# Retention attention and a mixture of adapters: each transfer of the SyncE queue waits for the landing of the third one ahead, and keys come in 256 KB pieces

## The chip, the cores and the metric

The kernel runs on one core of a Trainium2 chip. The metric is the device time of one execution in microseconds; lower is better. The median of the runs before the change is 192.85 us (three runs, 192.42 to 196.5).

## What is computed

The inputs are q, k and v of shape (8 batches, 8 heads, 576 positions, 64), all float32. Attention has no softmax; a decay per head takes its place:

```python
scores = q @ k.T / sqrt(64)                       # per batch and head, 576 x 576
D[i, j] = gamma[h] ** (i - j) if i >= j else 0    # gamma[h] = 1 - 2 ** (-5 - h)
x = (scores * D) @ v                              # heads laid side by side: 4608 rows of 512
logits = x @ w_gate                               # 8 experts, the best two are kept
out = x + sum over the two of w * ((x @ A[e]) @ B[e])     # A: 512 x 16, B: 16 x 512
```

Since D is a product of a factor of i and a factor of j, each block of rows needs only the keys and values of its own block and a 64 x 64 state per head that sums all earlier blocks.

## The kernel before

**Units.** The work is cut into 18 units (`units`). Units 0 to 15 are a pair of batches (bp) and a block c of 128 positions; units 16 and 17 are four batches each with the last 64 positions. The four units of one c come one after the other, so a state `SP[bp]` is used again four units later.

**Loads.** `load(u, w)` brings the tile of one unit from HBM into a buffer of `nt`: 512 KB for each of k, q and v. Before the change a key tile of units 1 to 15 is one transfer of 512 KB (line 160), values are two of 256 KB (line 148), queries from unit 2 on are two of 256 KB (line 153), and the tiles of units 16 and 17 are two of 256 KB each (line 144). Unit 0 comes in halves by batch (`load_batch`, line 538). Rows of k and v are 256 bytes in HBM; those of the paired q are 512. There are five buffers for q and six each for k and v.

**The SyncE queue.** All loads and nearly all stores are issued by SyncE, in the order in which the program writes them. First come units 0, 1 and 2, the expert weights (`AW`, lines 556 and 560: four transfers of 64 KB and one of 16 KB), and then units 3, 4 and 5. From then on `ahead(t)` sets the order:

```python
def ahead(t):
    for u in {4: (0,), 5: (1, 2)}.get(t, (t - 3,)):
        if t > 3 and has(u):
            store(u)                 # two stores of 256 KB, line 525
    for w in "kqv":
        load(t + 4, w)               # k, then q, then v
    if has(t + 1):
        first_state(t + 1)           # two copies on GpSimd, line 316
    if has(t + 2):
        scale_(t + 2, "k", pool2)    # line 179, GpSimd, one instruction a batch
        if t > 2:
            scale_(t + 2, "q", pool2)
```

The transfers before already carry a wait for the eighth one ahead of them, because eight semaphores are used in turn, and waits for their buffers.

**A round.** From t = 5 on each pass of the loop at the end does, on TensorE in this order: `scores(t)` (ps_s, line 269), `logits(t-1)` (pz, line 393), `small(t-2)` (pzt, line 378), `sums(t+1)` (pu, line 300), the transposes of k and q of unit t+1 (lines 215 and 202), `back(t-2)` (po, line 459), `products(t)` (px, line 350) and `output(t-2)` (po, line 475). GpSimd does `routing_4(t-2)` (cm and zc, lines 441 and 443) first, and then what `ahead(t)` gives it. ScalarE empties PSUM; VectorE masks. The engines' order is the program's; a semaphore wait at the head of an engine holds all that is behind it.

Of the kernel before, what the change touches and what calls it, by code (L numbers as in the profile page):

```python
# [18 lines left out]
def kernel(  # L19
# [10 lines left out]
    nc = tc.nc  # L30
    B, H, S, Dh = q.shape
# [31 lines left out]
    for c in range(NFULL):  # L63
# [9 lines left out]
    dr_pack2 = nc.inline_tensor(pack2_np, "c_pack2")  # L73
# [12 lines left out]
    pack2 = cpool.tile([128, NP2], FP32, tag="pack2", name="pack2", align_bytes=256)  # L86
# [14 lines left out]
        cpool.tile([128, 2, HP, Dh], FP32, tag=f"SP{bp}", name=f"SP{bp}") for bp in range(NP)  # L101
    ]

    units = [(c, bp) for c in range(NFULL) for bp in range(NP)] + [
        (NFULL, qd) for qd in range(NQ)
    ]
    NU = len(units)
# [4 lines left out]
    def paired(u):  # L112
        return 1 < u < NU and units[u][0] < NFULL
# [6 lines left out]
    def nt(u, w):  # L120
        if (u, w) not in nat:
            shape = [128, 2, 2 * H, Dh] if w == "v" else [128, 2 * H, Dh]
            nat[(u, w)] = iop.tile(
                shape, FP32, tag=w + "32", name=w + "32", bufs=5 if w == "q" else 6,
                align_bytes=256,
            )
        return nat[(u, w)]

    def block(u, t):
        return nt(u, "v")[:, t]  # L130

    def rows(w, b0, nb, s0, n):
        return SRC[w][b0 : b0 + nb, :, s0 : s0 + n, :].rearrange("b h j d -> j (b h) d")

    def load(u, w):
        if u >= NU:
            return
        c, bp = units[u]
        s0 = 128 * c
        if c == NFULL:  # L140
            for t in range(2):
                hf = slice(64 * t, 64 * t + 64)
                dst = block(u, t)[hf] if w == "v" else nt(u, w)[hf]
                nc.sync.dma_start(out=dst, in_=rows(w, 4 * bp + 2 * t, 2, s0, 64))
        elif w == "v":
            for t in range(2):
                hf = slice(64 * t, 64 * t + 64)
                nc.sync.dma_start(  # L148
                    out=block(u, t)[hf], in_=rows(w, 2 * bp, 2, s0 + 64 * t, 64)
                )  # L150
        elif w == "q" and paired(u):
            for b in range(2):
                nc.sync.dma_start(
                    out=nt(u, w)[64 * b : 64 * b + 64].rearrange("p (h e) d -> p h (e d)", e=2),
                    in_=q[2 * bp + b, :, s0 : s0 + 128, :].rearrange(
                        "h (p e) d -> p h (e d)", e=2
                    ),
                )
        else:
            nc.sync.dma_start(out=nt(u, w), in_=rows(w, 2 * bp, 2, s0, 128))  # L160

    def scale_(u, w, engines, bs=(0, 1)):
        c, _ = units[u]
# [356 lines left out]
    def store(u):  # L520
        c, bp = units[u]
        of = st.pop(u)["osb"].rearrange("p b a o d -> p b (a o d)")
        for b in range(2):
            if c < NFULL:
                nc.sync.dma_start(
                    out=o3[2 * bp + b, 128 * c : 128 * c + 128, :], in_=of[:, b]
                )
            else:
                for t in range(2):
                    (nc.gpsimd if b and u == NU - 2 else nc.sync).dma_start(  # L530
                        out=o3[4 * bp + 2 * t + b, 128 * c : 128 * c + 64, :],
                        in_=of[64 * t : 64 * t + 64, b],
                    )


    def load_batch(u, w, b):
        c, bp = units[u]
        nc.sync.dma_start(  # L538
            out=nt(u, w)[:, b * H : b * H + H], in_=rows(w, 2 * bp + b, 1, 128 * c, 128)
        )  # L540

# [4 lines left out]
    for b in range(2):  # L546
        for w in "kq":
            load_batch(0, w, b)
    load(0, "v")
    for w in "kqv":  # L550
        load(1, w)
    nc.sync.dma_start(out=pack2, in_=dr_pack2.ap())
    for w in "kqv":
        load(2, w)
    for dt in range(HP):
        nc.sync.dma_start(  # L556
            out=AW[:, dt, 0:ER].rearrange("p (e r) -> p e r", e=E),
            in_=moe_A[:, 128 * dt : 128 * dt + 128, :].rearrange("e d r -> d e r"),
        )
    nc.sync.dma_start(  # L560
        out=AW[:, :, ER : ER + E],
        in_=moe_w_gate.rearrange("(t p) e -> p t e", p=128),
    )
# [66 lines left out]
# [3 lines that stand above are left out]
                store(u)  # L633
        for w in "kqv":
            load(t + 4, w)
        if has(t + 1):
            first_state(t + 1)
        if has(t + 2):
            scale_(t + 2, "k", pool2)
            if t > 2:  # L640
                scale_(t + 2, "q", pool2)
# [51 lines left out]
    def finish():  # L693
        u = NU - 1
        s = st[u]
        store(u - 3)
        routing_4(u - 2)
        scores(u)
# [6 lines left out]
        routing_4(u - 1)  # L705
        products(u)
        store(u - 2)

        bv = Bcat.rearrange("p (a o d) -> p a o d", a=HP, o=2)
# [8 lines left out]
        for b in range(2):  # L718
# [10 lines left out]
                out=ns, in0=m8[:, 0:1], scalar=-1.0, in1=m8[:, 1:2],  # L729
# [3 lines left out]
                out=ge, in0=z[:, ER : ER + E],  # L733
# [3 lines left out]
                out=sg, in_=z[:, ER : ER + E], func=AFT.Sigmoid, bias=ns, scale=2.0  # L737
# [3 lines left out]
                out=c.rearrange("p (e r) -> p e r", e=E),  # L741
# [21 lines left out]
        def output_b(b, zt):  # L763
            o = mo.tile([128, HP, 2, 64], FP32, tag=f"oe{b}", name="oe", bufs=1, align_bytes=256)
            for ho, eng in ((0, nc.scalar), (1, nc.vector)):
                nc.tensor.matmul(
                    po[b][ho], lhsT=zt, rhs=bv[:, :, ho, :],
                    start=False, stop=True, skip_group_check=True,
                )
                (eng.copy if eng is nc.scalar else eng.tensor_copy)(  # L770
                    out=o[:, :, ho, :], in_=po[b][ho]
                )
            c, qd = units[u]
            of = o.rearrange("p a o d -> p (a o d)")
            for t in range(2):
                (nc.scalar if b and t else nc.sync).dma_start(
                    out=o3[4 * qd + 2 * t + b, 128 * c : 128 * c + 64, :],
                    in_=of[64 * t : 64 * t + 64],
                )

        zt0 = small_b(0)
        for b, tag in ((0, "s"), (1, "x")):
# [3 lines left out]
            for dt in range(HP):  # L786
                for ho in range(2):
# [3 lines left out]
                        is_transpose=True, start=(dt == 0), stop=False, skip_group_check=True,  # L791
                    )
        output_b(0, zt0)
        output_b(1, small_b(1))

    stage_A(2)
# [104 lines left out]
```

## Time and profile before

| | |
|---|---|
| median of the runs | 192.85 us (192.42 to 196.5, three runs) |
| profiled execution, its own time | 190.79 us |
| its span, first to last instruction | 188.9 us |
| granted TensorE clock, mean | 0.986 |
| busy: TensorE / VectorE / ScalarE / GpSimd | 167.3 / 113.3 / 114.1 / 108.7 us |
| HBM read, written | 29.02 MB, 9.44 MB |
| packets of the SyncE and ScalarE queues (q1) | 81.1% of 16 DMA engines' span |

The span is one execution as the hardware profiler recorded it; the execution's own time is 1.9 us longer, for what lies before the first and after the last instruction. "SPq" is SyncE's queue: its rows show how long each transfer held the issuing engine, which includes its waiting, and not how long the data took. A transfer's time to landing runs from the start of its issue to the last update of its semaphore.

### The profile page before, as it was taken

How to read it: one execution, taken by the hardware profiler on the slowest of the kernel's cores; microseconds unless marked ns; L12 is line 12 of the kernel's file. 1: busy time of each engine (PE TensorE's matmuls, PEld its weight loads, DVE VectorE, ACT ScalarE, POOL GpSimd, SP SyncE). 2: the span in 40 equal slices, each digit the busy share in tenths (PEclk: the TensorE clock that was granted, in tenths of full speed). 3: DMA queues.
4: the chain of work that ended last, by engine and by line, in shares of the span. 5: the costliest groups of instructions: out<-in, count | busy, mean ns of one | idle time of the engine just before them, and what ended most of it. 6: DMA issues, size and time to landing. Idle time of an engine off the chain costs nothing.

```text
span 188.9 us, 10441 instructions
## 1 busy us (share of the span) xinstructions
PE 167.3 (89%) x4675; PEld 148.9 (79%) x4675; DVE 113.3 (60%) x227; ACT 114.1 (60%) x255; POOL 108.7 (58%) x162
## 2 busy tenths in 40 slices
PE   3989598799889889898999999999997999999960
PEld 3578498588879788788999989899996988988840
DVE  1384837665296475748577787777594846555240
ACT  3437163735569484765767868494959394674650
POOL 1333321567769988493949586675969397520240
PEclk9999969999999999999999999999999999999998
DMA  7999969999999999999999999999998853112325
GB/s 157 248 221 225 227 70 232 202 224 246 224 228 235 262 252 277 252 260 247 241 257 246 266 232 250 221 278 226 271 206 243 181 169 115 50 68 111 115 56 166
DMA packets 108075, 38.99 MB, mean 206 GB/s; under 512 B 88768, under 2 KB 103488, under 8 KB 108032
## 3 DMA queue, kind: packets, MB, share of 16 engines
q1 hardware_dynamic: 107568, 37.71, 81.1%
q8 instruction: 36, 0.59, 1.4%
q0 software_dynamic: 240, 0.39, 1.0%
q10 hardware_dynamic: 224, 0.24, 0.5%
q14 instruction: 7, 0.06, 0.1%
HBM read 29.02 MB, written 9.44 MB: 204 GB/s over the span
## 4 chain that ended last, share of the span: by engine, by line
PE 59%; SPq 14%; issue 7%; DMA 6%; POOL 5%; DVE 4%; ACT 2%; POOLq 0%; ACTq 0%
PE px L350 15%; PE pz L393 12%; PE ps_s L269 8%; PE pu L300 6%; PE po L475 5%; PE po L459 4%; PE pt_k L215 4%; SPq L148 3%; SPq L556 3%; PE pt_q L202 3%; DMA k<-in_k_dram 3%; SPq L160 3%; DMA q<-in_q_dram 3%; POOL k L179 2%; SPq L538 2%
## 5 line engine op out<-in xcount | busy, mean ns | idle before, releaser
L179 POOL TENSOR_TENSOR k<-k,pack 128x512 f32<-128x512 f32 x32 | 34.9, 1109 | 17.4 <-DMA k<-in_k_dram 16.5
L350 PE MATMUL px<-x,v 128*64 128x64 f32 (+1 forms) x576 | 39.3, 226 | 2.6 <-DVE x L289 0.8
L289 DVE TENSOR_TENSOR x<-ps_s,pack 64x512 f32<-64x512 f32 (+1 forms) x38 | 25.1, 660 | 25.9 <-PE ps_s L269 25.6
L350 PE MATMUL px<-qT,v 128*64 128x64 f32 (+1 forms) x576 | 39.2, 226 | 1.3 <-DVE qT L289 1.1
L350 PEld LDWEIGHTS px<-x,v 128*64 128x64 f32 (+1 forms) x576 | 36.2, 140 | 4.4 <-ACT kT L240 1.0
L350 PEld LDWEIGHTS px<-qT,v 128*64 128x64 f32 (+1 forms) x576 | 36.1, 140 | 1.9 <-DVE qT L289 1.2
L393 PE MATMUL pz<-AW,xT 128*128 128x136 f32 x272 | 36.1, 286 | 0.6 <-ACT kT L240 0.6
L393 PEld LDWEIGHTS pz<-AW,xT 128*128 128x128 f32 x272 | 32.6, 190 | 1.8 <-ACT kT L240 0.8
L169 POOL TENSOR_TENSOR qs<-q,pack 128x512 f32<-128x512 f32 x25 | 26.1, 1062 | 4.1 <-DMA q<-in_q_dram 4.1
L406 ACT COPY zs<-pz 128x272 f32<-128x272 f32 x17 | 6.6, 386 | 33.2 <-PE pz L393 32.5
L289 DVE TENSOR_TENSOR qT<-ps_s,pack 64x512 f32<-64x512 f32 (+1 forms) x38 | 25.1, 660 | 1.1
L269 PE MATMUL ps_s<-qT,kT 64*64 64x64 f32 x1152 | 23.6, 224 | 2.1 <-issue 1.4
L269 PEld LDWEIGHTS ps_s<-qT,kT 64*64 64x64 f32 x1152 | 20.4, 137 | 6.2 <-issue 3.1
L441 POOL TENSOR_TENSOR cm<-ge,sg 128x16 f32<-128x16 f32 x17 | 4.0, 234 | 36.5 <-PE pt_k L215 16.9
L316 POOL COPY v<-SP 64x512 f32<-64x512 f32 x32 | 20.5, 640 | 1.6
L300 PE MATMUL pu<-v,k 64*64 64x64 f32 x1024 | 19.2, 221 | 0.8 <-DMA v<-in_v_dram 0.8
L240 ACT COPY kT<-pt_k 128x512 f32<-128x512 f32 x34 | 18.2, 589 | 1.2 <-PE pt_k L215 1.0
L253 DVE COPY x<-qT 64x512 f32<-64x512 f32 x17 | 14.5, 852 | 7.4 <-ACT qT L235 5.0
L366 ACT COPY xT<-px 128x512 f32<-128x512 f32 x28 | 16.3, 625 | 4.4 <-PE px L350 4.4
L300 PEld LDWEIGHTS pu<-v,k 64*64 64x64 f32 x1024 | 16.9, 134 | 2.5 <-DMA v<-in_v_dram 0.9
L492 ACT COPY osb<-po 128x512 f32<-128x512 f32 x33 | 17.6, 584 | 1.0 <-PE po L475 1.0
L252 DVE COPY x<-qT 64x512 f32<-64x512 f32 x14 | 8.1, 579 | 16.0 <-ACT qT L235 12.0
(68 smaller groups left out, 242.6 us busy)
## 6 DMA issues: line engine op xcount, KB each, us to landing
v<-in_v_dram SPq DMA_DIRECT2D x36, 256.0 KB, 5.2
q<-in_q_dram SPq DMA_DIRECT2D x34, 256.0 KB, 5.2
out_dram<-osb SPq DMA_DIRECT2D x32, 256.0 KB, 4.2
k<-in_k_dram SPq DMA_DIRECT2D x15, 512.0 KB, 5.7
k<-in_k_dram SPq DMA_DIRECT2D x6, 256.0 KB, 4.3
q<-in_q_dram SPq DMA_DIRECT2D x1, 512.0 KB, 6.9
out_dram<-oe SPq DMA_DIRECT2D x3, 128.0 KB, 3.3
AW<-in_moe_A_dram SPq DMA_DIRECT2D x4, 64.0 KB, 3.6
```

The costliest lines, as they stand in the source:

```text
L169: engines[b].tensor_tensor(out=qs[:, :, 4 * b : 4 * b + 4, :].rearrange("p e h d -> p h e d"), in0=tl[:, b * H : b * H + H, :].rearrange(" ...
L179: engines[b].tensor_tensor(out=tl[:, b * H : b * H + H, :], in0=tl[:, b * H : b * H + H, :], in1=g[:, c, :].unsqueeze(2).broadcast_to((128 ...
L240: nc.scalar.copy(out=tl[:, r], in_=st[u]["p" + w][r])
L253: eng.tensor_copy(out=x2[0:64, 1, b], in_=qT[64:128, 1, b])
L269: nc.tensor.matmul(ps[ho][64 * t : 64 * t + 64, b, hp, :], lhsT=kT[sl, t, b, hp, :], rhs=qT[sl, t, b, hp, :], start=(hp == 0 and b == bs[0 ...
L289: nc.vector.tensor_tensor(out=out, in0=in0, in1=m, op=ALU.mult)
L300: nc.tensor.matmul(pu[t][64 * ho : 64 * ho + 64, b, hp, :], lhsT=kn[sl, h, :], rhs=block(u, t)[sl, h, :], start=(hp == 0 and b == 0), stop ...
L316: copy(out=dst[:, :, :, ho, :], in_=src[64 * ho : 64 * ho + 64])
L350: nc.tensor.matmul(px[b][64 * ho : 64 * ho + 64, hp, t, :], lhsT=block(u, t)[rw, b * H + 2 * hp + ho, :], rhs=facing(u, t, ho)[rw, b, hp, ...
L366: nc.scalar.copy(out=xt.rearrange("p a (t i e) -> p (a t) e i", t=2, e=2), in_=px.rearrange("p a t (e i) -> p (a t) e i", e=2),)
L393: nc.tensor.matmul(pz[:, b, :], lhsT=st[u]["xT"][b][:, dt, :], rhs=AW[:, dt, :], start=(dt == 0), stop=(dt == HP - 1), skip_group_check=True,)
L492: copy(out=s["osb"][:, :, :, ho, :], in_=s["po"][ho])
```

## The change

A helper `move` issues every transfer of SyncE, keeps them in a list, and from the fourth on adds a wait for the landing of the transfer three places earlier in that list. So at most three transfers of this queue are on the way at a time. Key tiles (and the one q tile of unit 1 that takes the same branch) are issued as two transfers of 256 KB, one a batch, in place of one of 512 KB. Transfers issued by ScalarE (the first constants, one store at the end) and GpSimd (`Bcat`, two stores at the end) are not in the list.

```diff
+    inflight = []
+
+    def move(out, in_):
+        dma = nc.sync.dma_start(out=out, in_=in_)
+        if len(inflight) >= 3:
+            tc.add_manual_dep(
+                dma.ins, inflight[-3].ins.name,
+                mybir.DependencyInfo(mybir.DependencyClass.Sync, mybir.DependencyReason.DATA),
+                reason="pace",
+            )
+        inflight.append(dma)
...
         else:
-            nc.sync.dma_start(out=nt(u, w), in_=rows(w, 2 * bp, 2, s0, 128))
+            for b in range(2):
+                move(
+                    out=nt(u, w)[:, b * H : b * H + H], in_=rows(w, 2 * bp + b, 1, s0, 128)
+                )
...
             if c < NFULL:
-                nc.sync.dma_start(
+                move(
                     out=o3[2 * bp + b, 128 * c : 128 * c + 128, :], in_=of[:, b]
                 )
             else:
                 for t in range(2):
-                    (nc.gpsimd if b and u == NU - 2 else nc.sync).dma_start(
+                    (nc.gpsimd.dma_start if b and u == NU - 2 else move)(
```

All other `nc.sync.dma_start` calls become `move` in the same way. The order of instructions on TensorE, VectorE, ScalarE and GpSimd stays as it was. SyncE has 151 transfers in place of 135. In the changed program the instruction that scales the second batch of a key tile waits for the second key transfer alone, and the first for the first.

More of the change, by code (lines that the diff above doesn't have):

```diff
@@ L143, in load @@
                 dst = block(u, t)[hf] if w == "v" else nt(u, w)[hf]
-                nc.sync.dma_start(out=dst, in_=rows(w, 4 * bp + 2 * t, 2, s0, 64))
+                move(out=dst, in_=rows(w, 4 * bp + 2 * t, 2, s0, 64))
         elif w == "v":
@@ L152, in load @@
             for b in range(2):
-                nc.sync.dma_start(
+                move(
                     out=nt(u, w)[64 * b : 64 * b + 64].rearrange("p (h e) d -> p h (e d)", e=2),
@@ L159, in load @@
         else:
-            nc.sync.dma_start(out=nt(u, w), in_=rows(w, 2 * bp, 2, s0, 128))
+            for b in range(2):
+                move(
+                    out=nt(u, w)[:, b * H : b * H + H], in_=rows(w, 2 * bp + b, 1, s0, 128)
+                )
     def scale_(u, w, engines, bs=(0, 1)):
@@ L524, in store @@
             if c < NFULL:
-                nc.sync.dma_start(
+                move(
                     out=o3[2 * bp + b, 128 * c : 128 * c + 128, :], in_=of[:, b]
@@ L537, in load_batch @@
         c, bp = units[u]
-        nc.sync.dma_start(
+        move(
             out=nt(u, w)[:, b * H : b * H + H], in_=rows(w, 2 * bp + b, 1, 128 * c, 128)
@@ L551 @@
         load(1, w)
-    nc.sync.dma_start(out=pack2, in_=dr_pack2.ap())
+    move(out=pack2, in_=dr_pack2.ap())
     for w in "kqv":
@@ L555 @@
     for dt in range(HP):
-        nc.sync.dma_start(
+        move(
             out=AW[:, dt, 0:ER].rearrange("p (e r) -> p e r", e=E),
@@ L559 @@
         )
-    nc.sync.dma_start(
+    move(
         out=AW[:, :, ER : ER + E],
@@ L775, in output_b @@
             for t in range(2):
-                (nc.scalar if b and t else nc.sync).dma_start(
+                (nc.scalar.dma_start if b and t else move)(
                     out=o3[4 * qd + 2 * t + b, 128 * c : 128 * c + 64, :],
```

## The prediction

> **What bounds the kernel now.** I read the page first, then busy time by stage, the chain in order of time, SyncE's timeline and GpSimd's. The page:
>
> ```profile
> span 188.9 us, 10441 instructions
> PE 167.3 (89%) x4675; PEld 148.9 (79%) x4675; DVE 113.3 (60%) x227; ACT 114.1 (60%) x255; POOL 108.7 (58%) x162
> q8 instruction: 36, 0.59, 1.4%
> PE 59%; SPq 14%; issue 7%; DMA 6%; POOL 5%; DVE 4%; ACT 2%; POOLq 0%; ACTq 0%
> ```
>
> TensorE is busy 89% of the span, but a fifth of the chain that ended last (SPq and DMA) is transfers. Where these lie is shown by busy time in three stretches (columns: stretch, its length, then PE, PEld, DVE, ACT, POOL busy, granted clock, DMA share, GB/s) and by the chain (start, length, what):
>
> ```profile
> 0.00:55.00 55.00, 45.47 (x1232) 38.60 (x1232) 30.64 (x60) 26.71 (x58) 22.86 (x36) 0.97 0.96 209
> 55.00:150.00 95.00, 90.41 (x2711) 82.62 (x2713) 65.53 (x127) 65.24 (x144) 70.27 (x96) 1.00 0.98 244
> ...
> 26.74 5.68 DMA k<-in_k_dram
> 32.48 0.86 POOL k L179
> ...
> 44.00 5.15 DMA q<-in_q_dram
> ...
> 52.38 1.50 issue
> ...
> 109.47 1.10 PE ps_s L269 x64
> 118.02 0.49 PE ps_s L269 x18
> 121.61 0.11 PE pzt L378 x2
> ```
>
> Until some 50 us the chain runs through SyncE's queue and landings: the key issued at 26.74 lands at 32.42 and GpSimd scales it at 32.48. After 55 us it is TensorE alone, one round each 118.02 - 109.47 = 8.55 us. But the transfers are hardly slower than that, as a round of SyncE's queue shows (start, time that the issues held SyncE, what):
>
> ```profile
> 106.66 0.46 SPq L160 DMA_DIRECT2D k<-in_k_dram  x1
> 107.22 3.79 SPq L153 DMA_DIRECT2D q<-in_q_dram  x2
> 111.11 2.45 SPq L148 DMA_DIRECT2D v<-in_v_dram  x2
> 113.66 1.64 SPq L525 DMA_DIRECT2D out_dram<-osb  x2
> 115.34 0.46 SPq L160 DMA_DIRECT2D k<-in_k_dram  x1
> ...
> L153 SPq DMA_DIRECT2D q<-in_q_dram x28: 627/1436/3217, 15.4 to 127.7; - x28
> ```
>
> A round of transfers takes 115.34 - 106.66 = 8.68 us and SyncE never rests: a q issue takes 0.63 us unhindered and up to 3.2 us here. So the queue is full and transfers flow at 8.68 us a round against TensorE's 8.55. How far they are ahead is in GpSimd's timeline:
>
> ```profile
> 117.05 2.28 POOL L179 TENSOR_TENSOR k<-k,pack 128x512 f32<-128x512 f32 x2
> 119.29 2.04 POOL L169 TENSOR_TENSOR qs<-q,pack 128x512 f32<-128x512 f32 x2
> 123.56 0.22 POOL L441 TENSOR_TENSOR cm<-ge,sg 128x16 f32<-128x16 f32 x1 [2.23 <-PE pt_k L215]
> 123.86 0.77 POOL L443 TENSOR_TENSOR zc<-zs,cm 128x128 f16<-128x128 f32 x2
> ...
> k<-in_k_dram SPq DMA_DIRECT2D x15, 512.0 KB, 5.7
> v<-in_v_dram SPq DMA_DIRECT2D x36, 256.0 KB, 5.2
> q<-in_q_dram SPq DMA_DIRECT2D x34, 256.0 KB, 5.2
> out_dram<-osb SPq DMA_DIRECT2D x32, 256.0 KB, 4.2
> ```
>
> The key issued at 106.66 lands about 5.7 us later, at 112.4, and is scaled at 117.05: a lead of 4.7 us. Behind it GpSimd rests 2.2 us before cm, and that zc, done at 124.6, feeds the pzt of the next round, at 121.61 + 8.55 = 130.2: another 5.6 us. So keys and queries may come 4.7 + 2.2 + 5.6 = 12.5 us later, here, before TensorE waits. Before 50 us there is no such cover.
>
> **The change part by part.** *The wait.* Landing times of a round add up to 5.7 + 2 x 5.2 + 2 x 5.2 + 2 x 4.2 = 34.9 us; over 8.68 us that is 4.0 transfers on the way, 4.7 in pieces of 256 KB, since a key counts twice. The change allows three. Every transfer therefore starts at the same point or later than now, and with three on the way a transfer costs a third of its own landing time. That time in a window of three is not in the trace, but bounds are:
>
> ```profile
> L538 SPq DMA_DIRECT2D k<-in_k_dram x2: 448/894/1339, 0.7 to 1.9; - x2
> DMA to landing us min/median/max: 3.4/3.8/4.1
> ...
> L525 SPq DMA_DIRECT2D out_dram<-osb x32: 332/438/2492, 60.1 to 177.3; - x32
> DMA to landing us min/median/max: 2.0/4.2/6.0
> ```
>
> The very first load, with nothing ahead of it on this queue, lands in 3.4 us; in the full queue it is 5.2. I take 3.8, the median of the first burst, where one or two loads were ahead, as the window has it. A store lies between 2.0 (alone) and 4.2 (full queue); I take the middle, 3.1. A load then costs 3.8 / 3 = 1.27 us (1.13 to 1.73), a store 1.03 (0.67 to 1.40). A round of six loads and two stores takes (6 x 3.8 + 2 x 3.1) / 3 = 9.67 us, from 8.1 (below TensorE's 8.55, so hidden) to 13.2.
>
> [...]
>
> *The keys in two.* Sixteen more issues of about 0.45 us each, beside SyncE's waiting, cost nothing; without that cover 16 x 0.45 = 7.2 us. On the gain side, GpSimd may scale the first batch while the second lands. Where it waits for keys that saves one scaling, 1.0 us, in each of units 3 to 5; since these follow one another in one stream, once in all.
>
> ```profile
> 0.74 0.45 SPq L538 DMA_DIRECT2D k<-in_k_dram  x1
> ...
> 19.77 6.30 SPq L556 DMA_DIRECT2D AW<-in_moe_A_dram  x4
> 26.11 0.58 SPq L560 DMA_DIRECT2D AW<-in_moe_w_gate_dram  x1
> ...
> 42.31 2.33 SPq L153 DMA_DIRECT2D q<-in_q_dram  x2
> ...
> 60.10 2.97 SPq L525 DMA_DIRECT2D out_dram<-osb  x2
> ...
> 148.05 1.33 SPq L144 DMA_DIRECT2D v<-in_v_dram  x2
> ```
>
> *The stretch without cover.* Up to the second q of unit 5, issued by 44.64 us, there are 34 loads of 256 KB. Less 6.9 us for the five weight transfers (19.77 to 26.69), taken as unchanged, they came each (44.64 - 0.74 - 6.9) / 34 = 1.09 us. At 1.27 they end 34 x 0.18 = 6.1 us later. From this go 1.0 us for the split and the 1.5 us that the chain waits at 52.38 for something else, which leaves 3.6 us. GpSimd's stream holds cm and zc behind the late scalings, so TensorE is late next, at pzt.
>
> *The stretch with cover.* Fourteen more loads to 60.10 us add 14 x 0.17 = 2.4 us. Then ten rounds of loads to 149.38 us took 8.93 us each (eleven pairs of stores among them); in the window 9.67 + 0.21 for the eleventh pair = 9.88, so 9.5 us more. By unit 17 the loads are 6.1 + 2.4 + 9.5 = 18.0 us late. Of that 12.5 us are covered; 5.5 us reach TensorE, and the 3.6 us are part of them. Stores behind a waiting load wait with it; nobody waits for a store but three osb buffers, each free for rounds. The last stores wait for landings past by then: 0.
>
> *Sum.* The profiled execution took 190.79 us, its span and 1.9 us around it. 190.8 + 5.5 = 196.3. The median of the runs lies 2.06 us above this execution, so for the median 192.85 + 5.5 = 198.4 us.
>
> **The rivals.** *Window eats all the cover (chance 0.25).* The instruction queue's 36 packets are 0.59 MB / 36 = 16 KB each, on one DMA engine, and held it 0.014 x 16 x 188.9 / 36 = 1.2 us. Landing means all engines' parts landed, so each such packet may delay the issue of the next transfer in full, where a deeper queue let the others go on. With some two a round (36 over 17 rounds) and half of it unhidden, a round takes 9.67 + 1.2 = 10.9, ten rounds 10 us more: about 5.5 + 10 = 15.5, 208 us. It decides once a load's landing passes 3.95 us. For: in the full queue loads land in 5.2 us in the median, far above 3.8. Against: fewer transfers on the way should shorten each.
>
> *Hidden (0.22).* If a load lands in 3.4 us with three on the way, a round is 8.1 us, below TensorE's; the first stretch pays 34 x 0.04 = 1.4 us and gains 1.0 + 1.5. Result 192 to 193 us, no more than the median now. For it speaks that SyncE's issues are held for up to 3.2 us already, so the queue may be limited to about three as it is, and the new wait would do little. [...]
>
> *Faster (0.10).* TensorE has gaps in which nothing holds it that the profile shows, and these may be late instructions behind full data queues:
>
> ```profile
> PE po L459 <- issue: 1.5, 2, 0.9
> PE ps_s L269 <- issue: 1.4, 3, 0.8
> PE pt_q L202 <- issue: 0.5, 1, 0.5
> ```
>
> These are 3.4 us between 60 and 90 us. A shallower queue could remove them, and the split brings 1.0: 192.85 - 4.4 = 188.4 us, if transfers lose nothing. Against it: every transfer is issued no earlier than before.
>
> **How the numbers follow.** The forecast (0.43) is 198.4 us; by itself it spans 194 to 204 us, loads landing in 3.65 to 3.95 us. A measurement of this kernel can tell about 2%, 3.9 us, from no change. Slower by over 2%: the second rival's 0.25 and all but 0.07 of the forecast's, 0.61. Within 2%: that 0.07 and 0.22, 0.29. Faster by over 2%: 0.10. The range that leaves out no more than 2 in 10 takes in the hidden case and most of the window's: 190.5 to 210 us.
>
> **What would show it.** The round of SyncE's queue, from key to key, at 9.4 to 10.2 us; median landings of loads between 3.5 and 4.1 us; GpSimd waiting on landing keys and queries past 100 us; TensorE's round above 8.55 us towards the end; GB/s below 244 in the middle stretch. Wrong: a SyncE round at or below 8.7 us, or loads still landing in 5 us, or TensorE's gaps before 90 us gone.

## The result and the profile after

The changed kernel takes 210.8 us (median of four runs, 209.85 to 215.34) against 192.99 us for the kernel before (four runs, 192.42 to 196.5). The ratio is 1.092, with a 95% interval of 1.086 to 1.098: slower by 17.8 us, where 5.5 were forecast. Runs in which the chip was in its slower state are left out of all ratios here, which leaves the experiments paced_late and window5 one run each; the profiles of split_only, paced_late, window5 and window6 are of such slower runs.

The page of the changed kernel, to be laid beside the lines of the kernel before:

```profile
span 208.9 us, 10462 instructions
PE 177.4 (85%) x4675; PEld 157.1 (75%) x4675; DVE 109.5 (52%) x227; ACT 114.5 (55%) x255; POOL 108.4 (52%) x162
q8 instruction: 36, 0.59, 1.2%
DMA 65%; PE 20%; POOL 5%; issue 4%; SPq 2%; ACT 1%; DVE 0%; POOLq 0%; ACTq 0%
```

The chain that ended last was 59% TensorE; it is now 65% landings of transfers. Busy time by stage (stretch, length, PE, PEld, DVE, ACT, POOL busy, granted clock, DMA share, GB/s) shows it in the long middle one: 197 GB/s in place of 244.

```profile
55.00:150.00 95.00, 87.29 (x2524) 78.69 (x2524) 58.41 (x119) 60.49 (x134) 59.22 (x85) 0.98 0.76 197
```

SyncE's timeline (start, time that the issues held SyncE, what) has the keys of units 9 and 17 and the last pair of queries:

```profile
88.92 1.44 SPq L107 DMA_DIRECT2D k<-in_k_dram  x2
...
175.28 1.32 SPq L107 DMA_DIRECT2D k<-in_k_dram  x2
...
176.71 2.58 SPq L107 DMA_DIRECT2D q<-in_q_dram  x2
```

The same keys and queries in SyncE's timeline of the kernel before:

```profile
73.20 0.39 SPq L160 DMA_DIRECT2D k<-in_k_dram  x1
...
141.06 3.18 SPq L144 DMA_DIRECT2D k<-in_k_dram  x2
144.34 1.97 SPq L144 DMA_DIRECT2D q<-in_q_dram  x1
```

From the keys of unit 9 to those of unit 17 are eight rounds: (175.28 - 88.92) / 8 = 10.8 us each, before (141.06 - 73.20) / 8 = 8.5. The last queries go out 176.71 - 144.34 = 32.4 us later. Up to the last loads nearly every issue past the third starts 0.02 to 0.08 us after the landing of the third one ahead, or later where SyncE is still held by the issue before; so the wait is what paces the queue. What it paces is the time from issue to landing (count, size, median us):

```profile
k<-in_k_dram SPq DMA_DIRECT2D x36, 256.0 KB, 3.6
q<-in_q_dram SPq DMA_DIRECT2D x36, 256.0 KB, 4.2
v<-in_v_dram SPq DMA_DIRECT2D x36, 256.0 KB, 4.1
out_dram<-osb SPq DMA_DIRECT2D x32, 256.0 KB, 3.1
```

Loads landed in 5.2 us before, with more of them on the way; each is quicker now, but three at a time are too few. GpSimd's timeline shows that no lead is left:

```profile
119.47 0.76 POOL L458 TENSOR_TENSOR zc<-zs,cm 128x128 f16<-128x128 f32 x2
...
123.69 1.04 POOL L194 TENSOR_TENSOR k<-k,pack 128x512 f32<-128x512 f32 x1 [2.13 <-DMA k<-in_k_dram]
125.79 1.04 POOL L194 TENSOR_TENSOR k<-k,pack 128x512 f32<-128x512 f32 x1 [1.06 <-DMA k<-in_k_dram]
127.41 2.04 POOL L184 TENSOR_TENSOR qs<-q,pack 128x512 f32<-128x512 f32 x2 [0.58 <-DMA q<-in_q_dram]
```

Keys were scaled 4.7 us after their landing; now GpSimd waits 2.13 and 1.06 us for the two halves, zc comes late behind them, and TensorE waits for zc. Its waits (us in total, times, longest):

```profile
PE pzt L393 <- POOL zc L458: 10.9, 9, 2.8
PE pz L408 <- DMA AW<-in_moe_w_gate_dram: 2.3, 1, 2.3
...
PE ps_s L284 <- issue: 0.2, 1, 0.2
```

How late TensorE is, unit by unit, is read from the first matmuls of the scores of units 5, 8 and 17, in TensorE's timeline of the changed kernel and then of the kernel before:

```profile
66.90 1.15 PE L284 MATMUL ps_s<-qT,kT 64*64 64x64 f32 x61
...
93.71 0.99 PE L284 MATMUL ps_s<-qT,kT 64*64 64x64 f32 x52
...
190.58 1.16 PE L284 MATMUL ps_s<-qT,kT 64*64 64x64 f32 x64
```

```profile
61.67 1.15 PE L269 MATMUL ps_s<-qT,kT 64*64 64x64 f32 x60
...
92.22 1.20 PE L269 MATMUL ps_s<-qT,kT 64*64 64x64 f32 x60
...
170.87 1.16 PE L269 MATMUL ps_s<-qT,kT 64*64 64x64 f32 x64
```

Unit 5 is 5.2 us late, unit 8 only 1.5, unit 17 is 19.7. So the bill has three parts: a late start, 3.7 us made good between units 5 and 8, and then 18.2 us lost in nine rounds in which each unit waits for its transfers. The 3.7 us are nearly all idle spells that the profile calls issue, time in which TensorE waits for nothing that the profile shows: 3.4 us of them lie in this stretch of the kernel before (5.0 over the whole), 0.2 now.

### The profile page after: what moved, and what is told of

Read it like the earlier page. It is cut to its first block, busy times and chain, and to the rows that moved or that the text cites. A ratio compares the mean times of both kernels' runs of the same rounds, so it can differ in the third digit from the quotient of the medians.

```text
span 208.9 us, 10462 instructions
## 1 busy us (share of the span) xinstructions
PE 177.4 (85%) x4675; PEld 157.1 (75%) x4675; DVE 109.5 (52%) x227; ACT 114.5 (55%) x255; POOL 108.4 (52%) x162
## 4 chain that ended last, share of the span: by engine, by line
DMA 65%; PE 20%; POOL 5%; issue 4%; SPq 2%; ACT 1%; DVE 0%; POOLq 0%; ACTq 0%
DMA q<-in_q_dram 30%; DMA v<-in_v_dram 14%; DMA k<-in_k_dram 14%; PE px L365 6%; DMA out_dram<-osb 4%; PE pu L315 2%; POOL zc L458 2%; SPq L107 2%; POOL qs L184 2%; PE po L474 2%; PE pz L408 2%; DMA AW<-in_moe_A_dram 2%; PE po L490 2%; DMA pack<-c_pack 2%; PE ps_s L284 2%
## 5 line engine op out<-in xcount | busy, mean ns | idle before, releaser
L194 POOL TENSOR_TENSOR k<-k,pack 128x512 f32<-128x512 f32 x32 | 33.3, 1049 | 52.2 <-DMA k<-in_k_dram 51.7
L365 PE MATMUL px<-x,v 128*64 128x64 f32 (+1 forms) x576 | 41.8, 234 | 1.5 <-DVE x L304 0.7
L365 PE MATMUL px<-qT,v 128*64 128x64 f32 (+1 forms) x576 | 41.7, 234 | 1.1 <-DVE qT L304 1.1
L365 PEld LDWEIGHTS px<-x,v 128*64 128x64 f32 (+1 forms) x576 | 38.8, 148 | 3.5 <-DVE x L304 0.9
L365 PEld LDWEIGHTS px<-qT,v 128*64 128x64 f32 (+1 forms) x576 | 38.6, 148 | 1.6 <-DVE qT L304 1.2
L315 PE MATMUL pu<-v,k 64*64 64x64 f32 x1024 | 23.3, 237 | 2.6 <-DMA v<-in_v_dram 2.1
L255 ACT COPY kT<-pt_k 128x512 f32<-128x512 f32 x34 | 18.3, 590 | 12.5 <-PE pt_k L230 12.3
L315 PEld LDWEIGHTS pu<-v,k 64*64 64x64 f32 x1024 | 20.3, 149 | 4.8 <-issue 2.9
L267 DVE COPY x<-qT 64x512 f32<-64x512 f32 x14 | 8.6, 611 | 19.8 <-ACT qT L250 13.6
L230 PE MATMUL pt_k<-pack,k 64*128 64x64 f32 x288 | 15.7, 254 | 2.5 <-DVE k L194 2.0
L393 PE MATMUL pzt<-ident,zc 128*128 128x128 f16 x34 | 6.6, 227 | 12.2 <-POOL zc L458 10.9
```

The costliest lines, as they stand in the source:

```text
L194: engines[b].tensor_tensor(out=tl[:, b * H : b * H + H, :], in0=tl[:, b * H : b * H + H, :], in1=g[:, c, :].unsqueeze(2).broadcast_to((128 ...
L230: nc.tensor.matmul(ps[r][:, b, hp, :], lhsT=src[sl, b * H + 2 * hp : b * H + 2 * hp + 2, :], rhs=id64[sl, :], is_transpose=True, start=Tru ...
L255: nc.scalar.copy(out=tl[:, r], in_=st[u]["p" + w][r])
L315: nc.tensor.matmul(pu[t][64 * ho : 64 * ho + 64, b, hp, :], lhsT=kn[sl, h, :], rhs=block(u, t)[sl, h, :], start=(hp == 0 and b == 0), stop ...
L365: nc.tensor.matmul(px[b][64 * ho : 64 * ho + 64, hp, t, :], lhsT=block(u, t)[rw, b * H + 2 * hp + ho, :], rhs=facing(u, t, ho)[rw, b, hp, ...
```

## The experiments

**Which half of the change.** Two theories stood first. By one, a transfer costs the queue a fixed part, divided by the number on the way, and a part for its bytes. By the other, pieces as such are what costs.

```diff
 split_only: keys in two, no wait
-        if len(inflight) >= 3:
+        if False:
 wait_only: the wait, keys whole
-            for b in range(2):
-                move(out=nt(u, w)[:, b * H : b * H + H], in_=rows(w, 2 * bp + b, 1, s0, 128))
+            move(out=nt(u, w), in_=rows(w, 2 * bp, 2, s0, 128))
 window2, window4, window5, window6: the wait for the n-th one ahead
-        if len(inflight) >= 3:
-                dma.ins, inflight[-3].ins.name,
+        if len(inflight) >= 4:
+                dma.ins, inflight[-4].ins.name,
```

> Keys in two transfers of 256 KB, no added wait. Theory 'fixed part' (a transfer of 256 KB costs the queue about 2.0 us divided by the number on the way, plus 0.67 us that the DMA engines need for its bytes; both read off the changed kernel, where three landings lie 0.7 us apart and the next three come 4.0 us later): the number on the way is what it was before, so the median stays within 2% of the kernel before, 190 to 194 us, and SyncE's round stays at 8.6 to 8.8 us. Rival 'small pieces' (each further transfer costs a fixed 0.5 us or more whatever else is on the way): 15 more transfers, at least 7.5 us more by unit 17, visible as a SyncE round of 9.2 us and 195 us or more.

Measured: ratio 1.005 (1.000 to 1.010), 192.81 us. The split alone costs next to nothing.

> The wait for the third transfer ahead, keys in one transfer of 512 KB as before. Fixed part: a key costs 2.0/3 + 1.33 = 2.0 us in place of 2 x 1.33 = 2.67, so a round is 0.67 us shorter than the 10.8 us of the changed kernel, 10.1 us; over 15 keys some 10 us less, 199 to 203 us. Small pieces: the same direction but with the whole loss in the pieces, 192 to 195 us. Wait alone whatever the size (a transfer in a window of three takes the same time large or small): 16 keys x 1.33 us less, 188 to 194 us.

Measured: 202.29 us, ratio 1.050 (1.041 to 1.060), a round of (165.11 - 85.12) / 8 = 10.0 us. So the wait brings the loss, and the split makes it bigger only under the wait, where each half of a key takes a place in the window.

> As the changed kernel, but each transfer waits for the second one ahead. Fixed part: 2.0/2 + 0.67 = 1.67 us a transfer, 13.4 us a round (13 to 14); the second q of unit 17 lands at some 134 x 1.69 = 226 us and the end comes 26 us later: 245 to 260 us. If instead a landing always takes 4.05 us, whatever is on the way: 2.03 us a transfer, 16.2 us a round, about 300 us. Median landing of loads 3.1 to 3.5 us by the first, 4.0 by the second.

> As the changed kernel, but each transfer waits for the fourth one ahead. Fixed part: 2.0/4 + 0.67 = 1.17 us a transfer, a round of 9.3 to 9.5 us; the second q of unit 17 lands at some 134 x 1.19 = 160 us, 9 us later than in the kernel before, which its cover of some 12 us hides; 192 to 196 us. Rival 'instruction packets' (a packet of the instruction queue delays the landing of one transfer by 1.1 us and so the queue, two a round): a fourth transfer hides them, round at 8.6 us, 191 to 194 us. Rival 'coupling' (TensorE's pauses and lower clock feed back on the stores): a round above 10 us still, over 200 us.

SyncE's timeline in the window of two, and then of four, keys of units 9 and 17:

```profile
113.97 1.80 SPq L107 DMA_DIRECT2D k<-in_k_dram  x2
...
222.72 1.81 SPq L107 DMA_DIRECT2D k<-in_k_dram  x2
```

```profile
77.67 1.42 SPq L107 DMA_DIRECT2D k<-in_k_dram  x2
...
149.07 2.08 SPq L107 DMA_DIRECT2D k<-in_k_dram  x2
```

Rounds of 13.6 and 8.9 us, with 10.8 for three. Times the number on the way, over eight transfers, this is 3.4, 4.05 and 4.5 us for one transfer: some 2.2 us and 0.6 more for each one on the way, a fit to these three runs. Window2 took 262.03 us in its one run (245 to 260 expected). Window4 took 189.0 us, ratio 0.981 (0.973 to 0.989): faster than the kernel before, by 1 to 3%, and below the 192 to 196 that was expected. Coupling, as the rival had it, is out; the other two theories both survive, though neither expected so short a time.

**Why a landing takes 4.05 us.** The transfers alone, with the computing taken out, then with an instruction stream or with busy engines beside them.

```diff
 transfers_w3, transfers_free: all computing out, the same loads and stores in the same order
+                move(out=o3[2 * bp + b, 128 * c : 128 * c + 128, :], in_=src)
 transfers_pe: beside them
+    for _ in range(1160):      # x 4 matmuls, 64 x 64 tiles of zeros
+                nc.tensor.matmul(pf[r][64 * c : 64 * c + 64], lhsT=zero[sl, 0:64], rhs=zero[sl, 0:64], ...)
 transfers_vec: beside them
+    for eng, n in ((nc.vector, 180), (nc.scalar, 220), (nc.gpsimd, 105)):    # 128 x 512, own tiles
```

> The 151 transfers of SyncE in the order of the changed kernel, each waiting for the third one ahead, and nothing else: all computing is left out and the stores write a constant tile. Fixed part (windows of 2, 3 and 4 gave rounds of 13.7, 10.8 and 9.15 us, which is a landing of 2.2 us + 0.6 us for each transfer on the way): a round stays at 10.3 to 10.9 us, the second q of unit 17 lands near 178 us and the span is some 190 us. Instruction packets (the 36 packets of 16 KB and the computing slow the landings): without them loads land in 3.4 to 3.6 us, a round is 9.0 to 9.3 us and the span 160 to 168 us.

Its keys of units 9 and 17 in SyncE's timeline, and then the landings of its page:

```profile
79.63 1.42 SPq L107 DMA_DIRECT2D k<-in_k_dram  x2
...
153.94 1.32 SPq L107 DMA_DIRECT2D k<-in_k_dram  x2
```

```profile
k<-in_k_dram SPq DMA_DIRECT2D x36, 256.0 KB, 3.5
q<-in_q_dram SPq DMA_DIRECT2D x36, 256.0 KB, 3.8
v<-in_v_dram SPq DMA_DIRECT2D x36, 256.0 KB, 3.9
out_dram<-src SPq DMA_DIRECT2D x32, 256.0 KB, 2.3
```

A round of 9.3 us, at the upper end of what the second theory gave; the span of 177.7 us was off from both. Without the computing a load lands in 3.5 to 3.9 us and a store in 2.3.

> The 151 transfers alone with a window of three, as in the run where a round took 9.07 us (the kernel with all its computing takes 10.8), and beside them 4640 small TensorE matmuls on a tile of zeros, which wait for nothing: as many instructions to fetch as the kernel has, but no other engine at work and no data of the transfers read. All computing of the reference is left out. Theory 'instruction packets' (each 16 KB packet sits on one of the 16 DMA engines for about 1.1 us and holds the landing of one transfer, two packets a round): rounds of 10.2 to 10.9 us while the matmuls run, median landing of loads 4.0 us or more. Rival 'engines' traffic' (reading and writing on-chip memory slows the transfers): rounds stay at 9.0 to 9.3 us, loads at 3.5 to 3.9 us.

(The 9.07 us named there is the mean of five rounds of transfers_w3, from unit 10 to 15.) The keys of units 9, 14, 15 and 17 in SyncE's timeline, and then the page, with TensorE's busy time and the instruction queue:

```profile
92.78 1.02 SPq L107 DMA_DIRECT2D k<-in_k_dram  x2
...
147.02 1.91 SPq L107 DMA_DIRECT2D k<-in_k_dram  x2
...
158.17 1.02 SPq L107 DMA_DIRECT2D k<-in_k_dram  x2
...
176.90 1.32 SPq L107 DMA_DIRECT2D k<-in_k_dram  x2
```

```profile
PE 69.6 (35%) x4640; PEld 64.8 (32%) x4640; DVE 0.8 (0%) x2; POOL 0.2 (0%) x4
...
q8 instruction: 36, 0.59, 1.3%
...
q<-in_q_dram SPq DMA_DIRECT2D x36, 256.0 KB, 4.3
out_dram<-src SPq DMA_DIRECT2D x32, 256.0 KB, 3.3
```

> The same transfers with a window of three, and beside them 505 instructions of VectorE, ScalarE and GpSimd on 128 x 512 tiles of their own, over 100 us on each: much on-chip traffic, few instructions to fetch. All computing of the reference is left out. Instruction packets: rounds stay at 9.0 to 9.3 us. Engines' traffic: 10.2 to 10.9 us while these engines work, 9.1 us after they stop.

SyncE's timeline of that run:

```profile
80.19 1.27 SPq L107 DMA_DIRECT2D k<-in_k_dram  x2
...
155.31 1.32 SPq L107 DMA_DIRECT2D k<-in_k_dram  x2
```

The matmuls end at 151 us. While they run, from the keys of unit 9 to those of unit 14, a round takes (147.02 - 92.78) / 5 = 10.8 us; behind them, from unit 15 to 17, (176.90 - 158.17) / 2 = 9.4. With three busy engines and few instructions it is 9.4, alone 9.3. So a stream of instructions by itself brings the whole 1.5 us that the computing adds (10.8 - 9.3). This stream is somewhat denser than the kernel's: 23 of its packets start between 55 and 150 us, 20 in the changed kernel. The traffic of the other three engines is out as a cause.

How it does so is in the trace's list of semaphore updates: a transfer's semaphore is counted up in sixteen steps, and it has landed with the last. Of the loads issued between 55 and 150 us:

| run | loads | last step over 0.3 us behind the fifteenth | fifteenth step, us after the issue, mean | last step |
|---|---|---|---|---|
| changed kernel | 54 | 28 | 3.57 | 4.13 |
| transfers_pe | 52 | 28 | 3.72 | 4.18 |
| transfers_vec | 61 | 5 | 3.62 | 3.73 |
| transfers_w3 | 63 | 0 | 3.63 | 3.71 |

Fifteen steps come as early in the changed kernel as in the transfers alone; what is late is the last one, by 1.0 us on average in those 28 loads. An instruction packet holds one DMA engine for 1.1 us, so it fits; matmuls that slowed the on-chip memory would be expected to hold back more than one step of sixteen. Which engine each packet sat on, the trace does not tell.

> The same transfers alone, keys in two, without the added wait. Theory 'the queue is full' (the prediction's reading: in the kernel before transfers flow as fast as they can, 8.68 us a round): a round of 8.4 to 8.9 us, span 150 to 158 us. Theory 'the queue was paced by TensorE' (buffers that come free set the pace): 2.2/8 + 0.6 = 0.88 us a transfer, a round of 7.0 us, span 128 to 140 us.

Its span was 149.1 us and a round (127.82 - 65.86) / 8 = 7.7 us: between the two theories. Alone, the queue can do better than the 8.5 us of the kernel before; what it could do beside an instruction stream was not measured.

**Early loss or late rounds.**

```diff
 paced_first
-        if len(inflight) >= 3:
+        if len(inflight) >= 3 and len(inflight) < 42:
 paced_late
-        if len(inflight) >= 3:
+        if len(inflight) >= 3 and len(inflight) >= 42:
```

> The wait for the third transfer ahead only for the transfers up to the values of unit 5 (the first 42); keys in two throughout. Theory 'two separate bills': the scores of unit 5 come 5.2 us late as in the changed kernel; behind that the queue is free and TensorE sets the pace as before, with its idle spells of 'issue' back: 195 to 198 us. Theory 'all given back' (a late TensorE lets the queue get ahead, and later rounds are shorter): 191 to 194 us.

> The wait for the third transfer ahead only from the 43rd transfer on (keys of unit 6); the first 42 go without it, keys in two. Theory 'the queue sets the end' (from unit 9 on each unit starts when its keys and queries have landed, and the end comes 26 us after the last query): the 43rd transfer goes out some 5 us earlier than in the changed kernel, 91 more at 1.35 us each put the second q of unit 17 at 177 us, and the end at 203 us, 204 to 207 us with what lies around the span, although the scores of unit 5 are on time. Theory 'early loss and clock' (the changed kernel loses mainly before 60 us, by the late start and a halved TensorE clock): 195 to 199 us.

Paced_first: 200.4 us, ratio 1.040 (1.017 to 1.063), with 5.8 us of issue spells back. By the ratio it is some 7.6 us behind the kernel before on that chip (3.2 to 12.0 by the interval). In its profile the scores of unit 5 start 7.3 us later than before (68.99 against 61.67) and those of unit 17 8.3 us later (179.14 against 170.87): it gave nothing back. Paced_late: 205.99 us in its one comparable run, inside 204 to 207. In its profile, of a run of 209.89 us, the scores of unit 5 started at 63.22 us, near the 61.67 of before, and those of unit 17 at 190.13 us, as in the changed kernel. So an early TensorE does not help: the queue sets the end. That the first 42 transfers count in it by the 5 us that they hold up the rest of the queue fits the one comparable run; it was not shown further.

**Idle spells and depth.**

> Each transfer waits for the fifth one ahead. Fixed part: (2.2 + 5 x 0.6) / 5 = 1.04 us a transfer, a round of 8.4 us, under TensorE's 8.55: never late. If TensorE's idle spells of 'issue' come from a deep queue, they are between those of four (2.5 us) and of the split alone (6 us): 188.5 to 191 us. If four transfers on the way was just a lucky draw: 191 to 193 us.

> The window of four again, with keys in two, on another chip and in more rounds. Theory 'depth decides TensorE's idle spells' (5 to 7 us of spells that the profile calls issue with five or more transfers on the way, under 1 us with three): these spells at 2 to 5 us, ratio to the kernel before 0.975 to 0.995. Rival 'one lucky chip': ratio 0.995 to 1.02.

> The window of four with keys in one transfer of 512 KB: up to five pieces of 256 KB on the way, 0.5 us of a key's fixed part spared a round. By what a transfer costs, a round of some 8.6 us, below what TensorE needs with its spells; spells of issue between those of four and of five, 3 to 6 us: ratio 0.98 to 1.0. If the split of keys is what gains (units 3 to 5 start a key earlier): 0.995 to 1.01.

> A window of six, keys in two. Depth decides: spells of issue as without the wait, 5 to 7 us, and a queue that never limits: ratio 0.995 to 1.01. Rival 'any pacing gains': 0.975 to 0.99.

Window5 can't be compared: 194.2 us in its one usable run, against 191.07 and 193.51. The other three ran together on one chip: window4_again 0.986 (0.974 to 0.999), window4_whole 0.994 (0.989 to 0.999), window6 1.010 (0.999 to 1.021). The first of these has its ratio in the band of its first theory, though the interval reaches into that of the rival; the second cannot tell its two theories apart; in the third the rival is out. TensorE's idle spells in window4:

```profile
PE ps_s L284 <- issue: 2.0, 2, 1.4
PE px L365 <- issue: 0.5, 2, 0.3
```

| window, keys | spells of issue in the profile, us | ratio |
|---|---|---|
| 3, in two | 0.2 | 1.092 |
| 3, whole | 2.4 | 1.050 |
| 4, in two | 2.5 and 3.5 | 0.981 and 0.986 |
| 4, whole | 5.8 | 0.994 |
| 5, in two * | 7.2 | - |
| 6, in two * | 9.2 | 1.010 |
| none, in two * | 6.1 | 1.005 |
| none, whole (before) | 5.0 | 1 |

The starred rows rest on three of the profiles that are set apart in the section on the result, so growth past four is not shown. The other rows have 0.2 to 2.4 us with three, 2.5 to 5.8 with four and 5.0 in the kernel before.

What TensorE waits for in these spells can be read from the trace's list of packets: its instructions. In the kernel before each of the nine spells ends 1.3 to 1.6 us after the end of an instruction packet, though such packets end 4.8 us apart; the four spells of window4 and the seven of window4_again do the same. In transfers_pe, whose matmuls wait for no data, TensorE stands still 35 times, with 36 packets:

```profile
PE pf L565 <- issue: 79.5, 35, 3.2
```

Why there are fewer spells with fewer transfers on the way stays open. A packet took 1.1 us on average in the kernel before and in window4 alike, so it is not the packet itself that gets longer. A rival was not tested: where TensorE waits for data, as with three on the way, its instructions have time to arrive. The window of four with keys in two is the fastest measured, on two chips; whether by as much as 2% is open.

**One that failed.** The expert weights were issued by ScalarE, to shorten SyncE's queue, with the window of four.

```diff
 w4_aw, behind put_state(0, 1, ...)
-        move(out=AW[:, dt, 0:ER]..., ...)
+        nc.scalar.dma_start(out=AW[:, dt, 0:ER]..., ...)
```

> The window of four, and the five transfers of the expert weights issued by ScalarE behind its copies for unit 0 in place of SyncE. Until 50 us units wait for SyncE's queue, and units 3 and later now come five short transfers, 4 to 5 us, earlier in it; the pause of TensorE for these weights is gone too. Expected 0.96 to 0.975 of the kernel before, with the scores of unit 4 before 48 us (50.9 before). Rival 'TensorE and the other engines set the early rounds themselves': unit 4 at 50 us, ratio 0.975 to 0.99 as with the window of four alone. Rival 'ScalarE's issues hold up its evictions': above 0.99.

Measured: ratio 1.018 (1.009 to 1.026). ScalarE's timeline shows why:

```profile
14.41 1.72 ACTq L605 DMA_DIRECT2D AW<-in_moe_A_dram  x2
...
18.72 1.33 ACTq L609 DMA_DIRECT2D AW<-in_moe_w_gate_dram  x1
20.10 1.07 ACT L386 COPY xT<-px 128x512 f32<-128x512 f32 x2 [4.51 <-DMA AW<-in_moe_A_dram]
```

Five issues hold ScalarE for 5.6 us, and its eviction of px comes after an idle spell of 4.51 us. The scores of unit 1 start at 22.79 us, 4.1 later than in window4 (18.65), and those of unit 4 at 54.81, where 48 or less was expected. The third theory held.

## Why the prediction was wrong

**What failed is the size of a load's landing in the window.** The prediction took 3.8 us, from the first burst of the kernel before, and 3.1 for a store. From 72 to 175 us of the changed kernel loads took 4.14 us on average and stores 3.28, and issues started 0.12 us after the landing that freed them: (6 x 4.14 + 2 x 3.28 + 8 x 0.12) / 3 = 10.8 us, against the 9.67 forecast and just as measured. Of the 1.1 us between them, 0.7 are the loads, 0.1 the stores, and 0.3 the delay between a landing and the next issue, which the sum put at nothing. The working of the sum was right otherwise; its landing was that of transfers with few instructions beside them, as transfers_w3 shows (3.5 to 3.9 us), and the instruction stream lengthens it.

The prediction had just this as its rival "Window eats all the cover", with a round of 10.9 us and a time of 208, and gave it the smaller chance. Its mechanism is the one that the sixteen steps fit: one engine's late part holds the whole landing. Its number is right in part by luck: it put 1.2 us for the packets on top of 9.67, and the runs have 1.5 on top of 9.3. Its argument against, that fewer transfers shorten each, was true (5.2 us before) and did not suffice.

The Trainium skill, "DMA: Bandwidth & Descriptors", section "Why a DMA increments its semaphore by 16 and not by 1", says that a transfer runs on up to 16 engines which finish independently, and that only the full count means that all data has landed. The sixteen steps above agree: in 28 of 54 loads one step came late, and the landing with it.

**The queue's flow before.** "Transfers flow at 8.68 us a round" was read as what the queue can do. Alone it does 7.7 (transfers_free).

**The keys in two** were put at nothing for their issues, and split_only agrees (1.005). Under the wait they cost 210.8 - 202.3 = 8.5 us across two chips; the round of six loads held that price, but the part on the split did not tell it. The 1.0 us that the split was to bring units 3 to 5 does not show either: in window4, with keys in two as well, the scores of unit 5 start at 62.17 us, before the change at 61.67.

**The stretch without cover** was 6.1 us by the second query of unit 5: its issue came 6.8 us later (50.84 against 44.00), its landing 5.8 (54.97 against 49.15). That this is so near is in part luck. The issue of the expert weights was already 4.7 us late (24.51 against 19.77), the weights, taken as unchanged, added 1.1, and the sixteen loads behind them only 1.0. Of the 6.1 us 3.6 were to reach TensorE; 5.2 did. One item is missing there. TensorE paused 2.3 us for the expert weights, from 30.6 us on, and then its granted clock fell to half (columns as above, granted clock third from the end):

```profile
30.00:35.00 5.00, 2.72 (x58) 2.58 (x49) 4.14 (x6) 0.90 (x2) 0.00 (x0) 0.94 0.55 88
35.00:40.00 5.00, 4.53 (x68) 3.96 (x67) 1.22 (x5) 1.05 (x3) 3.04 (x3) 0.50 0.92 229
40.00:45.00 5.00, 4.60 (x136) 4.29 (x140) 1.23 (x1) 3.45 (x8) 2.88 (x4) 0.54 0.88 214
```

The Trainium skill, "TensorE: Matmul & The Clock Gate", section "Part 1: The HAM clock gate (the "warmup" mystery)", has the clock at half after an idle window of about 3.4 us. The half agrees; here the clock fell after one pause of 2.3 us, in a stretch of 5 us in which TensorE was busy for 2.72. How much of the 5.2 us this made was not measured by itself; the end was set by the queue all the same.

**The stretch with cover.** By the second values of unit 7 the issues were 11.4 us late (70.70 against 59.35), where 8.5 were forecast; the ten rounds behind added 21.0, where 9.5 were. So the queue was 32.4 us late by unit 17, in place of 18.0, and 11 of these 14.4 us are ten times the 1.1 us above. The cover of 12.5 us was right: the last queries go out 32.4 us later, the scores of unit 17 start 19.7 later, so 12.7 were covered.

**The rival "Faster"** had a true half. TensorE's issue spells did go (5.0 to 0.2 us), which the prediction had named as a sign that it would be wrong, but the time went the other way: by unit 9 the queue took over.

**The signs.** GpSimd's waits past 100 us, a TensorE round above 8.55 and GB/s below 244 came as said; a SyncE round of 9.4 to 10.2 did not (10.8), and the median landings, 3.6 to 4.2 us, reach just past the 3.5 to 4.1 that were named.

## What to carry to other kernels

A limit on the transfers on the way costs each transfer its landing time over that limit, so price it with landings measured beside the kernel's own instruction stream, and set the round against the engine that bounds it: here three gave 10.8 us against TensorE's 8.55, and four, with 8.9, were enough, since the loads' lead hid the rest. Cutting the keys in two cost next to nothing in the open queue (1.005) and some 8 us in the window of three, where each half takes a place. A somewhat shallower queue can be faster than an open one (0.981 and 0.986 with four); try the depth in both directions before judging it.

## What the runs showed that was not expected

- Some 4640 small matmuls on constant data lengthen other transfers' landings: query loads from 3.8 to 4.3 us, stores from 2.3 to 3.3, a round from 9.3 to 10.8. In 28 of 52 loads it is one late step of sixteen.
- TensorE's idle spells without a visible cause are waits for instructions: each of the nine in the kernel before ends 1.3 to 1.6 us after an instruction packet.
- In the window of three the landings often come in clumps, some 0.7 us apart, with a pause of 2 us or more between them (115.62, 116.37, 117.01, then 119.62, 120.34, 121.02 in the changed kernel).
- The granted clock was 0.50 and 0.54 in the ten microseconds that began 2 us after a pause of 2.3 us.
